# Attention and MLP in one launch: whole MLP products in the steps without maxima, residual sums on ScalarE and GpSimd, and maxima turned by DMA alone

## The chip, the cores and the metric

The kernel runs on one core of one Trainium2 chip. The core has TensorE (PE, matrix products), VectorE (DVE), ScalarE (ACT) and GpSimd (POOL), each with its own instruction queue, and SyncE (SP), whose queue issues nearly all DMAs. The metric is the device time of one execution in microseconds (us), the median of several runs.

## The reference

A pre-normalized transformer layer for 2048 tokens of width 512: 32 heads of 16, a softmax over all keys, then an MLP of width 1792 with SiLU.

```python
x = A_x
h = x + _A_ref(_layernorm(x, axis=-1), A_wqkv, A_wo)      # qkv, softmax(q k^T * scale) v, wo
h2 = h + _B_ref(_layernorm(h, axis=-1), B_w1, B_w2)       # silu(h @ w1) @ w2
return h2
```

## The kernel before, in words

**Items, steps, blocks.** The queries are cut into four blocks of 512. An item is one block with four heads, so there are 32 items (`i`), eight to a block. An item has 16 steps (`c`), one for each 128 keys; the loop at L1421 runs over all 512 steps (`g` = 16 i + c). In a step PE computes four score tiles (`scores`, L489: 128 keys by 512 queries, on one half of the array's rows, since a head's operands take 64 partitions), ACT takes their exponentials (`weigh`, into `pt`), and PE multiplies the exponentials of two steps earlier with the values (`values`, L887; LAG is 2), four heads side by side in 32 columns each. The last item (`LAST`, i = 31) is split otherwise: its first eight steps treat two heads, its last eight the other two.

**Maxima.** The softmax needs an upper bound per query. So each score is computed a second time, with queries on partitions, and DVE reduces each 128x512 tile to its maxima (`maximum`, L291, reduce at L307). There are 64 such tiles per item, 2048 in all, and they run some items ahead of the scores. They use the half of PE's rows that a score leaves free. When all of an item's maxima (a piece; in the last item a piece is half an item) are found, `finish_max` (L314) reduces them further and splits them into two fp16 rows on DVE and POOL. Then the rows must be turned (transposed) and copied into the rows of `qs`. There are two ways. `place_far` (L350) turns by a DMA (SP) and copies by two DMAs a step later. `place_max` (L368) turns on PE, copies out of PSUM on DVE, and copies by two DMAs a step later. `found_maxima` (L414) chooses: far pieces take `place_far`, near ones are put into `late` and take `place_max`. A piece is near if its first step is at most 3 steps away, at most 6 in the items of FIRSTS, or if it is a half piece of the last item. While a piece is in `late`, `maxima` (L1390) allows one maximum less in that step (`late_now`).

**Order.** All engines' instructions keep the order of the program text. `maxima(g)` decides how many maxima a step takes: 3 in most steps; in the steps of `beside` 4, or 5 where fewer than 64 + 4 (g + LEAD) are done, with LEAD 4. Callbacks wait in `agenda` (`soon(n, fn)` runs fn n steps later, at the step's start).

**The output stages.** In items 8, 16 and 24 (FIRSTS) the block just finished is projected with wo, in steps c = 9 to 15 (`output`, L1261, with n = c - 9). For n < 4 it multiplies the rows of a fourth of the block with wo (12 whole-row products into one PSUM bank, with three more maxima, MORE, after the sixth), adds x on DVE (`add_rows`, L1075), takes the statistics (`statistics`, L222: two DVE operations, then two small POOL operations for `rs`, 1/sigma), normalizes the rows of the call before on DVE (into `hx`), and splits normalized rows into a high and a low fp16 half (`split_normal`, L1081: copy on ACT, low half on POOL, for the last rows on DVE). `turn_beside` (L131) turns both halves into `hts` by a DMA on SP. Besides, `split_rows` (L1043) prepares the next rows of the attention's output in c = 10 and 11, a copy on ACT and a low half on POOL, ahead of `output`.

**The MLP beside the attention.** For the first three blocks the MLP runs in the steps of `beside`: 112 steps from the fifth step (c = 4) of the item after the output stage, or to the end, 404 to 511, for the third. Products are cut into halves of 64 rows (`half_product`, L1187), so that one half of the array works on the MLP and the other on scores or maxima (`beside_products`, L1212): on even steps the upper half of a product, on odd steps the lower half, 6 (or 7) per step. A chain of products fills one PSUM bank: 12 for each of 14 slices of the first matrix, 42 for each of four row groups of the second. In the third block the last two chains have 7 per step, so that the chain of rows 2 runs in steps 488 to 499 and that of rows 3 in 500 to 511. When a chain ends, ACT copies the bank (`g`), and later steps do the rest on ACT and POOL. Scores then have three PSUM banks, maxima three.

**The end.** After the last step `finish_last` (L1288) finishes the last item and does the fourth block's projection and MLP alone.

The functions that the diff touches, and what calls them:

Of the kernel before, what the change touches and what calls it, by code (L numbers as in the profile page):

```python
# [10 lines left out]
F32 = mybir.dt.float32  # L11
# [9 lines left out]
P = 128  # L21
# [70 lines left out]
def attention_mlp_kernel(ctx: ExitStack, tc: tile.TileContext, x, wqkv, wo, w1, w2, out):  # L92
# [19 lines left out]
    def act(fn, *a, **k):  # L112
        ins = getattr(nc.scalar, fn)(*a, **k)  # L113
        pin(ins)
        return ins

    def after(ins, earlier):

        tc.add_manual_dep(ins.ins, earlier.ins.name, mybir.DependencyInfo(
            mybir.DependencyClass.Sync, mybir.DependencyReason.DATA), reason="row halves in one bank")  # L120

    def dve(fn, *a, **k):
        pin(getattr(nc.vector, fn)(*a, **k))  # L123
# [4 lines left out]
    def dma(*a):  # L128
        pin(nc.sync.dma_start(*a))
# [155 lines left out]
    def start_of(piece):  # L285
        i, a = piece
        return KC * i + HALF * (a or 0)
# [61 lines left out]

    def place_far(piece):  # L350

        i, _ = piece
        mt = small.tile([P, P], F16, name="mt", bufs=1)
        pin(nc.sync.dma_start(mt, wide.pop(piece), transpose=True))
        split.pop(piece)

        def out():
            for j in range(2):
                rows = qs[i % RING][64 * j + 48:64 * j + 50].rearrange("r a n -> r (a n)")
                dma(rows.rearrange("r (a b) -> r a b", b=P), mt[16 * j:16 * j + 16, :])  # L360
            placed.add(piece)

        if at["attention"]:
            soon(1, out)
        else:
            out()
# [22 lines left out]
                           key=lambda t: (t[1], t[3]) if i < 2 else t[3])  # L389
            for i in range(ITEMS) for j in range(2)}  # L390
    END = 64 * ITEMS
    at = {"item": 0, "done": 0, "half": 0, "step": 0, "due": 0, "attention": False, "group": None, "ready": 0, "next": 0, "piece": 0, "blocks": True}
    agenda, late = {}, {}

    def soon(steps, fn, *a):

        agenda.setdefault(at["step"] + steps, []).append((fn, a))
# [16 lines left out]
    def found_maxima(piece):  # L414
        g = at["group"]
        output = g is not None and g // KC in FIRSTS
        if g is None or piece[1] is None and start_of(piece) - g > FAR + 3 * output:
            soon(WAIT + 1 if g is None else CALM if g > FIRSTS[0] * KC else CALM + 1, place_far, piece)
            finish_max(piece, g is not None and g > FIRSTS[0] * KC)
            return  # L420
        late.setdefault(at["step"] + (1 if output else WAIT), []).append(piece)
        unfinished.append(piece)
        found_at["step"] = at["step"]

# [61 lines left out]
    def pt_tile(name, second, dtype=F32):  # L486
        return bp.tile([P, 512], dtype, tag=f"pt{second}", name=name, bufs=PTS[second])

    def scores(g, k, kind="st"):  # L489

        i = g // KC
        a, j, c = head(g, k)
        assert piece_of(i, a) in placed
        ps = bank(kind)
        mm(ps, ks[i % RING][64 * j:64 * j + 64, a, c * P:(c + 1) * P], qs[i % RING][64 * j:64 * j + 64, a, :],
           start=True, stop=True)

        def weigh():
            pts[g, k] = pt_tile("pt", g % 2 if g in beside else k // 2)
            return act("activation", pts[g, k], ps, AF.Exp, scale=qk_f)  # L500

        return weigh
# [569 lines left out]
    def rows_of(b, t):  # L1072
        return ot[b % 2][:, t].rearrange("p c n -> p (c n)")

    def add_rows(b, t, ps):  # L1075

        dve("scalar_tensor_tensor", rows_of(b, t), ps, wo_f, hx[t], op0=ALU.mult, op1=ALU.add)

    halves = {}

    def split_normal(t):  # L1081
        rows, halves[t] = hx.pop(t), gates[:, FC - 4 + t]
        act("copy", halves[t][:, 0], rows)
        low(halves[t][:, 1], rows, halves[t][:, 0], "pool" if t < 3 else "dve")

    def gate(ps, engine="dve"):
        g, parts = zp.tile([P, 512], F32, name="g"), parts_of(pt_tile("gh", 1))
# [99 lines left out]
    def half_product(j):  # L1187
# [10 lines left out]
            after(ins, current.pop("fence"))  # L1198
        current["half"][j] += 1

    def imbalance(left, side, others, same):

        rest = [left[j] - (same if j == side else others) for j in range(2)]
        worst = max(0, -min(rest))
        while sum(rest) > 0:
            side = 1 - side
            rest[1 - side] -= 3
            rest[side] -= 1
            worst = max(worst, -min(rest) if sum(rest) >= 0 else 0)
        return worst  # L1210

    def beside_products(g, n):  # L1212

        if not current:
            count, share, of, end = chains.pop(0)
            current.update(count=count, share=share, of=of, end=end, half=[0, 0], open=[], gone=0)
# [24 lines left out]
        for m in range(max(len(other), len(same))):  # L1241
            for kind, x in same[m:m + 1] + other[m:m + 1]:
                if kind == "score":
                    weigh = scores(*x)
                    if current.get("fence", True) is None:
                        current["fence"] = weigh()
                    else:
                        weigh()
                elif kind == "max":
                    one_max(x)  # L1250
                elif kind == "half":
                    half_product(x)
# [7 lines left out]

    def output(b, n):  # L1261

        if n < 4:
            ps = bank()
            weave(project_rows(n, ps), {6: lambda: singles(MORE[n])})
            add_rows(b, n, ps)
        t = n - 3
        if t in halves:
            turn_beside(hts, slice(t * P, (t + 1) * P), halves.pop(t))
        t = n - 2  # L1270
        if 0 <= t < 4:
            split_normal(t)
            if t == 3:
                turn_beside(hts, slice(t * P, (t + 1) * P), halves.pop(t))
        if 0 < n < 5:
            normalize(hx[n - 1], rows_of(b, n - 1), *found.pop(n - 1))

        if n < 4:
            found[n] = statistics(rows_of(b, n), LN)

    O = ot[(NB - 1) % 2]

# [138 lines left out]
    for g in range(groups):  # L1421
# [45 lines left out]
        at["group"] = g  # L1467
        n = maxima(g)

        if g in beside:  # L1470
            beside_products(g, n)
        else:
            half = 1 - head(g, g % 2)[1]
            j = next_item()
            more = len(todo[j, half]) - len(todo[j, 1 - half]) if j < ITEMS else 0
            slots = range(n)
            if n == 3 and more < 0:
                slots = range(1, 4)
# [55 lines left out]
```

## Time and profile before

| | |
|---|---|
| median of 3 runs | 1562.98 us (1562.96 to 1563.38) |
| the profiled execution | 1562.87 us, span 1561.1 us |
| mean granted TensorE clock | 1.000 |
| DVE, maxima of one tile (L307) | 1842, 1146.7 us, 683 ns each |
| ACT, exponentials (pt) | 2048, 1049.1 us, 607 ns each |
| PE, scores | 2048, 639.7 us |
| PE, scores for maxima | 2048, 671.9 us |
| PE, values (pt, va) | 4096, 538.6 us |
| PE, half products of the MLP | 1008 + 1008 |

How to read it: busy time of one engine overlaps that of the others, and matmuls overlap each other (0.38 us each, but a new one can begin every 0.2 us). A duration of an instruction on DVE, ACT or POOL also contains its start, which overlaps the end of the one before; what one more costs is the distance from start to start. The chain of waits goes back from the last instruction, at each step to what released it, and so says which engine set the time in each stretch. A merged row, "x4", stands for four instructions in a row. In the rows `L99` is the helper of all matmuls, `L113` that of all ACT operations, `L123` and `L106` those of DVE and POOL, so that tiles tell operations apart: `w<-ot,mv,rs` is the normalization in an output stage, `ot<-ps,factors,w` the sum with x, `st` and `mv` the statistics, `rs` 1/sigma, `gates<-w,gates` the low half of normalized rows (`gates<-ot,gates` of the attention's output), `ps<-qs,ks` a score tile (64*128) and `ps<-ks,qs` one for the maxima (48*128), `ps<-w,gates` a half product.

### The profile page before, as it was taken

How to read it: one execution, taken by the hardware profiler on the slowest of the kernel's cores; microseconds unless marked ns; L12 is line 12 of the kernel's file. 1: busy time of each engine (PE TensorE's matmuls, PEld its weight loads, DVE VectorE, ACT ScalarE, POOL GpSimd, SP SyncE). 2: the span in 40 equal slices, each digit the busy share in tenths (PEclk: the TensorE clock that was granted, in tenths of full speed). 3: DMA queues.
4: the chain of work that ended last, by engine and by line, in shares of the span. 5: the costliest groups of instructions: out<-in, count | busy, mean ns of one | idle time of the engine just before them, and what ended most of it. 6: DMA issues, size and time to landing. Idle time of an engine off the chain costs nothing.

```text
span 1561.1 us, 30995 instructions
## 1 busy us (share of the span) xinstructions
PE 1548.6 (99%) x11483; PEld 500.0 (32%) x11483; DVE 1376.0 (88%) x2188; ACT 1232.9 (79%) x2404; POOL 553.8 (35%) x761
## 2 busy tenths in 40 slices
PE   9999999999999999999999999999999999999999
PEld 6433322222222333333322333333322333332354
DVE  7999999999999999999999999999999999993322
ACT  6545799999977889888868998888868989888532
POOL 6643444554532354311142544310142445211100
PEclk9999999999999999999999999999999999999999
DMA  6667423333433122344433211444432221335322
GB/s 219 171 171 234 140 80 96 99 112 94 119 89 93 31 57 61 108 128 142 141 78 86 57 45 49 129 141 130 120 97 69 56 62 48 91 107 172 97 88 75
DMA packets 136260, 163.18 MB, mean 105 GB/s; under 512 B 43312, under 2 KB 80240, under 8 KB 136108
## 3 DMA queue, kind: packets, MB, share of 16 engines
q1 hardware_dynamic: 131356, 152.68, 33.9%
q10 hardware_dynamic: 4752, 8.52, 2.0%
q8 instruction: 90, 1.47, 0.4%
q14 instruction: 62, 0.51, 0.1%
HBM read 126.48 MB, written 24.63 MB: 97 GB/s over the span
## 4 chain that ended last, share of the span: by engine, by line
PE 88%; DVE 8%; ACT 2%; issue 1%; POOL 0%; POOLq 0%; ACTq 0%
PE ps L99 87%; DVE mx L307 5%; ACT pt L113 1%; DVE mx L305 1%; PE ps L102 1%; DVE w L123 0%; DVE st L123 0%; DVE ot L123 0%; DVE pvs L123 0%; POOL wv_l L106 0%; ACT g L113 0%; ACT pvs L113 0%; DVE xtl L123 0%; DVE ks L123 0%; POOL rs L106 0%
## 5 line engine op out<-in xcount | busy, mean ns | idle before, releaser
L307 DVE TENSOR_REDUCE mx<-ps 128x1 f32<-128x512 f32 x1842 | 1146.7, 683 | 58.7 <-PE ps L99 26.5
L113 ACT ACTIVATE pt<-ps 128x512 f32<-128x512 f32 x2048 | 1049.1, 607 | 179.3 <-PE ps L99 177.4
L99 PE MATMUL ps<-ks,qs 48*128 48x512 f16 x2048 | 671.9, 380 | 5.2 <-DVE mx L307 2.4
L99 PE MATMUL ps<-qs,ks 64*128 64x512 f16 x2048 | 639.7, 377 | 0.6
L99 PE MATMUL ps<-pt,va 128*17 128x512 f32 x4096 | 538.6, 598 | 0.6
L99 PE MATMUL ps<-hts,w 64*128 64x512 f16 (+2 forms) x1212 | 285.0, 372 | 0.0
L99 PE MATMUL ps<-w,gates 64*128 64x512 f16 x1008 | 245.6, 378 | 0.1
L99 PEld LDWEIGHTS <-ks 64*128 64x128 f16 x2048 | 177.0, 94 | 207.6 <-issue 163.2
L99 PEld LDWEIGHTS <-qs 48*128 48x128 f16 x2048 | 167.1, 94 | 69.1 <-issue 29.2
L99 PEld LDWEIGHTS <-w 64*128 64x128 f16 (+1 forms) x1212 | 101.6, 95 | 236.9 <-ACT pt L113 107.2
L99 PEld LDWEIGHTS <-gates 64*128 64x128 f16 (+1 forms) x1152 | 95.1, 94 | 240.2 <-ACT pt L113 112.7
L106 POOL TENSOR_TENSOR ri<-rc,minus 128x16 f32<-128x16 f32 x31 | 90.7, 2926 | 220.8 <-DMA rc<-dn 220.8
L99 PEld LDWEIGHTS ps<-pt,va 128*17 128x17 f32 x4096 | 68.2, 95 | 204.1 <-issue 196.3
L305 DVE TENSOR_REDUCE mx<-ps 128x2 f32<-128x1024 f32 x103 | 119.1, 1219 | 4.3 <-PE ps L99 3.5
L106 POOL TENSOR_SCALAR t<-t,factors 128x512 f32<-128x512 f32 x42 | 29.1, 693 | 190.5 <-ACT t L113 190.5
L113 ACT ACTIVATE g<-ps,factors 128x512 f32<-128x512 f32 x68 | 47.0, 692 | 42.6 <-PE ps L99 42.6
L106 POOL TENSOR_TENSOR ot<-ot,g 128x512 f32<-128x512 f32 x12 | 15.3, 1272 | 122.5 <-ACT g L113 122.5
L113 ACT ACTIVATE ks<-ps 128x512 f32<-128x512 f32 x30 | 17.9, 597 | 50.2 <-PE ps L99 43.9
L123 DVE SCALAR_TENSOR_TENSOR gh<-g,factors,gh 128x512 f16<-128x512 f32 x14 | 10.5, 751 | 52.1 <-ACT gh L113 52.1
L106 POOL TENSOR_TENSOR t<-t,g 128x512 f32<-128x512 f32 x42 | 53.7, 1278 | 3.5
L106 POOL TENSOR_TENSOR sl<-ks,sh 128x512 f16<-128x512 f32 x30 | 34.6, 1155 | 50.5 <-ACT sh L113 32.2
L106 POOL TENSOR_SCALAR nm<-nm 128x16 f32<-128x16 f32 (+1 forms) x42 | 10.8, 257 | 112.4 <-DVE nm L321 108.2
(160 smaller groups left out, 1025.7 us busy)
## 6 DMA issues: line engine op xcount, KB each, us to landing
w<-w2d SPq DMA_DIRECT2D x182, 256.0 KB
ks<-kd SPq DMA_DIRECT2D x120, 192.0 KB
w<-w1d SPq DMA_DIRECT2D x56, 256.0 KB
ks<-in_B_w_dram ACTq DMA_DIRECT2D x28, 256.0 KB
w<-in_B_w_dram SPq DMA_DIRECT2D x28, 256.0 KB
qs<-qd SPq DMA_DIRECT2D x128, 48.0 KB
kd<-sh SPq DMA_DIRECT2D x16, 256.0 KB
qd<-sh SPq DMA_DIRECT2D x16, 256.0 KB
```

The costliest lines, as they stand in the source:

```text
L99: return tc.keep_in_program_order(nc.tensor.matmul(*a, **k))
L102: tc.keep_in_program_order(nc.tensor.transpose(*a))
L106: tc.keep_in_program_order(getattr(nc.gpsimd, op)(*a, **k))
L113: ins = getattr(nc.scalar, fn)(*a, **k)
L123: pin(getattr(nc.vector, fn)(*a, **k))
L305: pin(nc.vector.tensor_reduce(of, space[:, n:n + 2, :], axis=AX.X, op=ALU.max))
L307: pin(nc.vector.tensor_reduce(of[:, j:j + 1], space[:, n, :], axis=AX.X, op=ALU.max))
```

## The change

Three things. (1) In `found_maxima` the choice goes by distance alone (more than 3 steps), so that half pieces and near pieces of the output stages take `place_far`, in an output stage one step after they are found. (2) In `output` ACT multiplies the projected rows by wo_f into SBUF and POOL adds x, behind the normalization of the rows before (`after`); the statistics of these rows move to the start of the next call; the last rows are normalized one call later, split two calls later (their turn comes in the next item's first step); the halves of rows 2 and 3 are copied by POOL, not ACT, and all low halves are POOL's. (3) In the steps of `beside` where no maxima are left and the current product is complete in both halves, `beside_scores` issues the step's four scores and then as many whole-row products as spread the rest evenly over the steps left (all but the last); two of the maxima's PSUM banks go to the scores.

```diff
@@ found_maxima
-        if g is None or piece[1] is None and start_of(piece) - g > FAR + 3 * output:
-            soon(WAIT + 1 if g is None else CALM if g > FIRSTS[0] * KC else CALM + 1, place_far, piece)
+        if g is None or start_of(piece) - g > FAR:
+            soon(WAIT + 1 if g is None else 1 if output else CALM if g > FIRSTS[0] * KC else CALM + 1, place_far, piece)
             finish_max(piece, g is not None and g > FIRSTS[0] * KC)
             return
-        late.setdefault(at["step"] + (1 if output else WAIT), []).append(piece)
+        late.setdefault(at["step"] + WAIT, []).append(piece)
@@ place_far
-        i, _ = piece
+        i, a = piece
+        n = 16 if a is None else 8
...
-                rows = qs[i % RING][64 * j + 48:64 * j + 50].rearrange("r a n -> r (a n)")
-                dma(rows.rearrange("r (a b) -> r a b", b=P), mt[16 * j:16 * j + 16, :])
+                rows = qs[i % RING][64 * j + 48:64 * j + 50, slice(None) if a is None else slice(a, a + 1)]
+                dma(rows.rearrange("r a n -> r (a n)").rearrange("r (a b) -> r a b", b=P), mt[n * j:n * j + n, :])
@@ weigh
-            pts[g, k] = pt_tile("pt", g % 2 if g in beside else k // 2)
+            pts[g, k] = pt_tile("pt", g % 2 if g in beside and not at["alone"] else k // 2)
@@ split_normal
-        act("copy", halves[t][:, 0], rows)
-        low(halves[t][:, 1], rows, halves[t][:, 0], "pool" if t < 3 else "dve")
+        if t < 2:
+            act("copy", halves[t][:, 0], rows)
+        else:
+            pool("tensor_copy", halves[t][:, 0], rows)
+        low(halves[t][:, 1], rows, halves[t][:, 0], "pool")
@@ new
+    def whole_products(count):
+        for _ in range(count):
+            lhs, rhs = next(current["of"])
+            ins = mm(space[:, at["bank"], :], lhs, rhs, start=current["half"] == [0, 0], stop=current["half"][0] == current["count"] - 1)
...
+            current["half"] = [n + 1 for n in current["half"]]
+            current["gone"] += 1
+        if current["gone"] == current["count"]:
+            current["end"](space[:, at["bank"], :])
+            current.clear()
+
+    def beside_scores(g):
+
+        if not current:
+            begin_chain()
+        rest = current["count"] - current["gone"] + sum(count for count, *_ in chains)
+        groups_left = max(beside) - g
+        for k in range(4):
+            scores(g, k ^ (g % 2))()
+        whole_products(min(current["count"] - current["gone"], -(-rest // groups_left)))
@@ output
+        if 0 < n < 5:
+            found[n - 1] = statistics(rows_of(b, n - 1), LN)
         if n < 4:
             ps = bank()
             weave(project_rows(n, ps), {6: lambda: singles(MORE[n])})
-            add_rows(b, n, ps)
+            if n:
+                mv, rs = found.pop(n - 1)
+                norm = nc.vector.tensor_scalar(hx[n - 1], rows_of(b, n - 1), mv[:, 0:1], rs, op0=ALU.subtract, op1=ALU.mult)
+                pin(norm)
+            z = zp.tile([P, 512], F32, name="g")
+            act("mul", z, ps, wo_f)
+            add = nc.gpsimd.tensor_tensor(rows_of(b, n), z, hx[n], ALU.add)
+            pin(add)
+            if n:
+                after(add, norm)
         t = n - 3
         if t in halves:
-            turn_beside(hts, slice(t * P, (t + 1) * P), halves.pop(t))
-        t = n - 2
-        if 0 <= t < 4:
+            turn_half(t)
+        for t in {2: (0,), 3: (1,), 4: (2,), 6: (3,)}.get(n, ()):
             split_normal(t)
             if t == 3:
-                turn_beside(hts, slice(t * P, (t + 1) * P), halves.pop(t))
-        if 0 < n < 5:
-            normalize(hx[n - 1], rows_of(b, n - 1), *found.pop(n - 1))
-
-        if n < 4:
-            found[n] = statistics(rows_of(b, n), LN)
+                soon(1, turn_half, t)
+        if n == 5:
+            normalize(hx[3], rows_of(b, 3), *found.pop(3))
+
+    def turn_half(t):
+        turn_beside(hts, slice(t * P, (t + 1) * P), halves.pop(t))
@@ the loop over steps
-        if g in beside:
+        if g in beside and next_item() == ITEMS and (at["alone"] or current and current["half"][0] == current["half"][1]):
+            if not at["alone"]:
+                at["alone"] = True
+                banks["st"] += banks["sm"][:2]
+                banks["sm"] = banks["sm"][2:]
+            if chains or current:
+                beside_scores(g)
+            else:
+                for k in range(4):
+                    scores(g, k ^ (g % 2))()
+        elif g in beside:
             beside_products(g, n)
```

More of the change, by code (lines that the diff above doesn't have):

```diff
@@ L119, in after @@
         tc.add_manual_dep(ins.ins, earlier.ins.name, mybir.DependencyInfo(
-            mybir.DependencyClass.Sync, mybir.DependencyReason.DATA), reason="row halves in one bank")
+            mybir.DependencyClass.Sync, mybir.DependencyReason.DATA), reason="order")
     def dve(fn, *a, **k):
@@ L391, in attention_mlp_kernel @@
     END = 64 * ITEMS
-    at = {"item": 0, "done": 0, "half": 0, "step": 0, "due": 0, "attention": False, "group": None, "ready": 0, "next": 0, "piece": 0, "blocks": True}
+    at = {"item": 0, "done": 0, "half": 0, "step": 0, "due": 0, "attention": False, "group": None, "ready": 0, "next": 0, "piece": 0, "blocks": True, "alone": False}
     agenda, late = {}, {}
@@ L1073, in rows_of @@
         return ot[b % 2][:, t].rearrange("p c n -> p (c n)")
-    def add_rows(b, t, ps):
-        dve("scalar_tensor_tensor", rows_of(b, t), ps, wo_f, hx[t], op0=ALU.mult, op1=ALU.add)
     halves = {}
@@ L1199, in half_product, with begin_chain @@
         current["half"][j] += 1
+    def whole_products(count):
+        for _ in range(count):
+            lhs, rhs = next(current["of"])
+            ins = mm(space[:, at["bank"], :], lhs, rhs, start=current["half"] == [0, 0], stop=current["half"][0] == current["count"] - 1)
+            if "fence" in current:
+                after(ins, current.pop("fence"))
+            current["half"] = [n + 1 for n in current["half"]]
[11 more added lines that the diff above has]
+        whole_products(min(current["count"] - current["gone"], -(-rest // groups_left)))
+    def begin_chain():
+        count, share, of, end = chains.pop(0)
+        current.update(count=count, share=share, of=of, end=end, half=[0, 0], open=[], gone=0)
     def imbalance(left, side, others, same):
@@ L1214, in beside_products @@
         if not current:
-            count, share, of, end = chains.pop(0)
-            current.update(count=count, share=share, of=of, end=end, half=[0, 0], open=[], gone=0)
+            begin_chain()
         side = g % 2
```

## The prediction

> **What bounds the kernel now.** I read the page first, then the chain of waits, then the timelines of the stretches that the diff touches.
>
> ```profile
> span 1561.1 us, 30995 instructions
> PE 88%; DVE 8%; ACT 2%; issue 1%; POOL 0%; POOLq 0%; ACTq 0%
> ```
>
> TensorE (PE) carries the end almost everywhere, VectorE (DVE) for 8% of the span, ScalarE (ACT) for 2%. POOL (GpSimd) is as good as never on the chain. So work moved to POOL or ACT is worth something only in the DVE pieces of the chain, and PE work removed is worth its own time. The profiled execution took 1562.87 us, 1.77 more than its span and 0.11 below the median; I sum differences and take them from the median 1562.98. About 0.2% (3.1 us) is what a measurement can tell from no change.
>
> A step is one pass of the loop over g; c is its number within an item. Each step shows as a burst of four exps on ACT, so bursts mark steps. The three output stages (blocks 1, 2, 3 in order of time) project rows in c9 to c12, finish the normalization after that, and begin the MLP beside the attention at c4 of the next item.
>
> ```profile
> 454.87 2.07 ACT L113 ACTIVATE pt<-ps 128x512 f32<-128x512 f32 x4 [3.31 <-PE ps L99]
> 471.81 2.06 ACT L113 ACTIVATE pt<-ps 128x512 f32<-128x512 f32 x4 [3.15 <-PE ps L99]
> 487.66 3.08 DVE mx L307 x5
> 801.69 2.06 ACT L113 ACTIVATE pt<-ps 128x512 f32<-128x512 f32 x4 [3.31 <-PE ps L99]
> 818.52 2.06 ACT L113 ACTIVATE pt<-ps 128x512 f32<-128x512 f32 x4 [2.81 <-PE ps L99]
> 835.09 1.29 DVE mx L307 x2
> 1147.44 2.07 ACT L113 ACTIVATE pt<-ps 128x512 f32<-128x512 f32 x4 [3.31 <-PE ps L99]
> 1164.04 2.07 ACT L113 ACTIVATE pt<-ps 128x512 f32<-128x512 f32 x4 [2.81 <-PE ps L99]
> 1180.61 1.29 DVE mx L307 x2
> ```
>
> In each block the first row is c10, the second c13, the third the first reduce of c4. So c10 to c12 take 16.94, 16.83 and 16.60 us, and the seven steps c13 to c3 take 15.85, 16.57 and 16.57. From c4 on, as the chain's row for block 1 shows, a step costs five reduces of DVE, 3.08.
>
> **c10 to c12, the row sums.** What PE needs alone is seen at the start of block 3's stage, before DVE falls behind (upper rows of the timeline of PE; the lower ones are a step near the end of the attention):
>
> ```profile
> 1142.71 0.59 PE L99 MATMUL ps<-wo_h,gates 128*128 128x512 f16 x2
> 1143.36 0.59 PE L99 MATMUL ps<-wo_h,gates 128*128 128x512 f16 x2
> 1143.79 0.38 PE L99 MATMUL ps<-wo_l,gates 128*128 128x512 f16 x1
> 1144.10 0.60 PE L99 MATMUL ps<-ks,qs 48*128 48x512 f16 x3
> 1144.63 0.60 PE L99 MATMUL ps<-wo_h,gates 128*128 128x512 f16 x2
> 1148.09 0.59 PE L99 MATMUL ps<-wo_h,gates 128*128 128x512 f16 x2
> ...
> 1441.41 0.39 PE L99 MATMUL ps<-w,gates 64*128 64x512 f16 x1
> 1442.71 0.38 PE L99 MATMUL ps<-w,gates 64*128 64x512 f16 x1
> 1443.02 1.05 PE L99 MATMUL ps<-pt,va 128*17 128x512 f32 x8
> 1444.03 0.39 PE L99 MATMUL ps<-w,gates 64*128 64x512 f16 x1
> ```
>
> From projection to projection it is 1148.09 − 1142.71 = 5.38, with whole-row products 0.215 apart (two between 1143.36 and 1143.79). Three such steps are 16.14, so DVE costs 0.80, 0.69 and 0.46 there. What DVE does is shown by block 2 at the end of c12, and in c13 and c14:
>
> ```profile
> 817.41 0.74 DVE L123 SCALAR_TENSOR_TENSOR ot<-ps,factors,w 128x512 f32<-128x512 f32 x1
> 818.07 0.54 DVE L123 TENSOR_SCALAR w<-ot,mv,rs 128x512 f32<-128x512 f32 x1
> 818.52 0.69 DVE L123 BATCH_NORM_STATS2 st<-ot 128x6 f32<-128x512 f32 x1
> 819.24 0.18 DVE L123 BATCH_NORM_AGGREGATE mv<-st 128x2 f32<-128x6 f32 x1
> 819.34 1.85 DVE L307 TENSOR_REDUCE mx<-ps 128x1 f32<-128x512 f32 x3
> 821.11 1.50 DVE L123 TENSOR_SCALAR w<-ot,mv,rs 128x512 f32<-128x512 f32 x1
> 822.53 1.88 DVE L307 TENSOR_REDUCE mx<-ps 128x1 f32<-128x512 f32 x3
> 824.33 0.68 DVE L123 TENSOR_TENSOR gates<-w,gates 128x512 f16<-128x512 f32 x1
> 824.93 0.68 DVE L307 TENSOR_REDUCE mx<-ps 128x1 f32<-128x512 f32 x1
> ```
>
> By start-to-start spacing a step has six reduces (2 × 1.8 = 3.6), the sum 0.66, the normalization 0.45 and the statistics 0.82: 5.5, over PE's 5.38. Without the sum it is 4.9, and PE becomes the bound at 5.38. The sum's new way:
>
> ```profile
> L113 ACT ACTIVATE g<-ps,factors 128x512 f32<-128x512 f32 x68 | 47.0, 692 | 42.6 <-PE ps L99 42.6
> L106 POOL TENSOR_TENSOR ot<-ot,g 128x512 f32<-128x512 f32 x12 | 15.3, 1272 | 122.5 <-ACT g L113 122.5
> L106 POOL CAST gates<-t 128x512 f16<-128x512 f32 x42 | 25.6, 610 | 2.7
> ```
>
> It takes 0.69 on ACT and 1.27 on POOL, 2.0 after the projection. Its reader, the statistics, now stands behind the next step's three reduces, about 2.9 after the projection (values 1.01, from 1443.02 to 1444.03, then 1.85 of reduces), so the sum is hidden by some 0.9. ACT stands idle 2.8 to 3.3 before each burst in those rows, so its 0.69 costs nothing. The sum on POOL waits for the normalization before it; behind it in POOL's queue lie a low half (one of the costs below) and the next two small operations for 1/sigma, which the next normalization needs 1.9 or more after the statistics. The tightest place is c11, where split_rows puts a low half ahead of them: I find about 0.1 to spare. If that cover is gone, DVE waits and PE with it (a rival below). I take the whole 0.80 + 0.69 + 0.46 = **2.0**; bounds 0 and 2.0.
>
> **c13 to c3, the end of the normalization.** Counted from c13's first exp (818.52), the reduces of c13 begin 0.8 late now, since sum, normalization and statistics stand ahead of them. After the change that 0.8 is gone, but the statistics (0.82) stand behind these reduces instead: nothing won. The low half on DVE, 0.60 by spacing (824.33 to 824.93), goes to POOL: 0.6 won. The normalization of the last rows is the costly one: 1.50 rather than 0.54. POOL tells why:
>
> ```profile
> 819.51 0.19 POOL L106 TENSOR_SCALAR rs<-mv 128x1 f32<-128x1 f32 x1 [2.56 <-DVE mv L123]
> 819.79 0.56 POOL L106 TENSOR_TENSOR rs<-rs,expos 128x1 f32<-128x1 f32 x1
> 821.17 1.16 POOL L106 TENSOR_TENSOR gates<-w,gates 128x512 f16<-128x512 f32 x1 [0.82 <-ACT gates L113]
> ```
>
> It lies beside a low half on POOL and both end together. After the change, counted from c13's exps: reduces 0.05 to 1.85, statistics, mv at 2.57, 1/sigma on POOL to 3.7, the copy that came from ACT (0.61) to 4.35, low half from 4.45 to 5.6. On DVE the next reduces run from 2.67, so the normalization starts at 4.45 as well. They meet again, and it stays 1.5. So blocks 2 and 3 win 0.6 each. Block 1 escapes the collision today, and one reduce is missing in its c13:
>
> ```profile
> 473.81 0.53 DVE L123 TENSOR_SCALAR w<-ot,mv,rs 128x512 f32<-128x512 f32 x1
> ```
>
> Its 15.85 becomes the others' 16.0: 0.1 lost. Sum **1.1**; bounds −0.4 (each block's 0.6 eaten, block 1 at 16.3) and 3.9 (no collision).
>
> The Trainium skill, page "SBUF — State Buffer", section "Who interferes with whom", has it that such a DVE operation and a GpSimd one take a shared port pair in turn, and that the first to issue holds it. By that rule a normalization that starts first would keep its 0.54 (1551.2 as the sum). The trace does not bear it out: at 821.11 the normalization started 0.06 ahead of POOL and still paid.
>
> Two things move on SP's queue. The last rows' halves are turned by DMA in c0 rather than c14; c4, which reads them, comes four steps of 2.3 (16.0 / 7) later, 9 us: free, and if it is not, c4's first products wait. The turned maxima now pass SP twice, the second time behind the turn of rows 1, which waits for POOL's low half. In block 1 they are issued about 5 us after c13's exps; c0 begins at 6, but DVE's late reduces hold its last maximum until 8, so that I take them as covered. Uncovered they cost up to 1 in block 1.
>
> **Maxima.** A piece that waited to be turned by TensorE took one maximum out of a step (late_now). Each output stage then started the MLP one short and paid one more five-reduce step. Now 3.08 instead of 2.62 (tail rows below, also seven slots) for one step less per block: 3 × 0.46 = **1.4**. The same hiccup before the end:
>
> ```profile
> 1398.55 2.07 ACT L113 ACTIVATE pt<-ps 128x512 f32<-128x512 f32 x4 [0.55 <-PE ps L99]
> 1401.70 1.09 ACT L113 ACTIVATE pt<-ps 128x512 f32<-128x512 f32 x2 [1.08 <-PE ps L99]
> ```
>
> That step is 3.15 where its neighbours are 2.6: **0.5**. The turns' own work on PE and DVE lies inside these differences.
>
> **The tail.** By the target in the code (64 + 4 × (g + 4) maxima before step g) all 2048 are done at step 492, which leaves twenty steps. A step there (the lower PE rows) is seven half products at 0.217, with four scores in the other half of the array, 0.31 to the values, 1.01 to the next step: 2.62. After: four scores in pairs (2 × 0.215), a change to whole rows, n products at 0.215, values. The change to whole rows is priced by the three 48-row maxima at 1144.10, which fill two slots: 1144.63 − 1144.10 − 0.215 = 0.31, or 0.09 over a slot. With n = 4: 0.215 + 0.31 + 0.645 + 0.31 + 1.01 = 2.49; with n = 3: 2.27. Left at step 492 are 28 + 42 products over 19 steps, each taking the rest divided by the steps left, rounded up: n = 4 in 13 steps, 3 in six, none in the last. That wins 13 × 0.13 + 6 × 0.35 = 3.8. ACT needs 2.06 per step and now has 0.2 to 0.4 left for two evictions of 0.69 and a copy: 0.1 to 0.2 worse. The last step saves 1.1 on PE, but its values wait for its exps: 0.4. Five score banks let each step's scores go out at once. Sum **4.0**; bounds 1.5 (each step at 2.6) and 5.
>
> The Trainium skill, page "TensorEngine Tiling (Array Packing)", section "Key Properties", warns that changing the tiling mode drains TensorE, which speaks against this part. The trace agrees with 0.09 a change; were the drain a whole matmul's 0.38, 19 more of them would take back 5.5.
>
> **Sum.** 2.0 + 1.1 + 1.4 + 0.5 + 4.0 = 9.0: 1562.98 − 9.0 = **1554.0**.
>
> **The rivals.**
> *No collision*: the normalization gets in ahead of POOL's low half or between copy and low half. 0.95 per block more, −11.8: 1551.2. For it: the tie is 0.01 us by my sums. Against: both collisions on record. 20%.
> *The tail gives little*: ACT's queue or the scores' banks hold each step near 2.55, or whole products are not entered at step 492 because a product is half done (against this: 14 of 42 are done on both sides). −5 to −6.5: about 1557. 17%.
> *GpSimd becomes the bound* (the slower side): POOL's order puts a sum (1.27) or low half ahead of 1/sigma, and each of the three following normalizations of a block waits x. It costs 9x; from x = 1.0 the gain is gone, at a whole sum and its gap, 1.4, it gives −9.0 + 12.6: 1566.6. For it: c11's 0.1. Against: POOL is idle 2.6 us before 1/sigma in the row. 6%.
> *No change*: PE binds the output stages anyway and half the tail is lost: −1 to −3, about 1561. 6%.
>
> **How the numbers follow.** The forecast has 51%. The range 1550.5 to 1558.0 takes in the first two rivals; the slower and the unchanged case stay outside. Faster by over 0.2%: 0.51 + 0.20 + 0.17 = 0.88; same 0.06; slower 0.06.
>
> **What would show it.** Right: c10 to c12 at 5.38 a step with no DVE in the chain; one five-reduce step less in each block; bursts at 2.49 and 2.27 in the tail; normalizations of 1.5 in c14. Wrong: DVE waiting for rs in c11, scores of c0 waiting for a DMA on qs, bursts still 2.6 apart after the last reduce, or a span above 1559.

## The result and the profile after

| | before | after |
|---|---|---|
| median | 1563.02 us (1562.92 to 1563.38, 6 runs) | 1553.76 us (1553.58 to 1554.09, 6 runs) |
| ratio after / before, 95% interval | | 0.9941 [0.9928, 0.9954] |
| profiled execution, and its span | 1562.87 us, 1561.1 us | 1553.58 us, 1551.7 us |

The change saves 9.26 us; the forecast was 1554.0. The page of after answers the two lines of before:

```profile
span 1551.7 us, 30864 instructions
PE 91%; DVE 6%; ACT 2%; issue 1%; POOL 0%; DMA 0%; SPq 0%; POOLq 0%; ACTq 0%
```

VectorE's share of the chain has fallen from 8% to 6%, TensorE has taken it over, and neither GpSimd nor ScalarE carries more of it. The chain of waits through the output stage of block 1 shows where DVE went (short pieces of "issue" between the rows are left out):

```profile
450.24 5.35 PE ps L99 x30
455.62 5.35 PE ps L99 x30
460.99 5.35 PE ps L99 x30
466.37 4.74 PE ps L99 x25
471.13 1.89 DVE mx L307 x3
...
475.61 2.24 DMA qs<-mt
477.90 2.73 PE ps L99 x17
...
486.93 3.08 DVE mx L307 x5
```

The steps c10 to c12 are pure PE at 5.38 from start to start, with nothing of DVE between them. ACT's part of the sum (`g`) has gone into the idle time of 3.31 that stood ahead of c10's exps: 2.08 are left ahead of `g`, and 0.55 between `g` and the exps (timeline of ACT):

```profile
453.73 0.69 ACT L113 ACTIVATE g<-ps,factors 128x512 f32<-128x512 f32 x1 [2.08 <-PE ps L99]
454.97 2.06 ACT L113 ACTIVATE pt<-ps 128x512 f32<-128x512 f32 x4 [0.55 <-PE ps L99]
```

In the chain a new link has come in: PE waits for the copy of the turned maxima (`qs<-mt`) before c0 can begin. Block 2 has one exception, in c12, where the chain goes through ACT:

```profile
809.87 0.69 ACT g L113
810.55 0.51 ACT gates L113
811.06 0.51 ACT pt L113
811.61 9.47 PE ps L99 x58
```

`g` and a copy stand ahead of the step's exps there, and the step takes 5.51 rather than 5.38. The same two stand there in blocks 1 and 3, where the step takes 5.38. In block 3 `g` starts 0.48 after the start of the projection's last product (1153.25 to 1153.73), in block 2 0.76 after it (809.11 to 809.87); what held it there the profile does not show.

In the groups of instructions, kept apart by shape, the normalization splits into the nine that `output` issues under a projection and the three of the last rows, issued in c14 (columns: busy us, mean ns of one, idle before):

```profile
L1295 DVE TENSOR_SCALAR w<-ot,mv,rs 128x512 f32<-128x512 f32 x9 | 4.9, 540 | 0.6 <-POOL rs L106 0.5
L123 DVE TENSOR_SCALAR w<-ot,mv,rs 128x512 f32<-128x512 f32 x3 | 4.0, 1320 | 0.0
```

The last rows still pay, 1.32 rather than 0.54. In the tail, the timeline of PE shows the new steps: four scores, then four or three whole-row products, then the values.

```profile
1438.85 1.05 PE L99 MATMUL ps<-pt,va 128*17 128x512 f32 x8
1439.84 0.60 PE L99 MATMUL ps<-qs,ks 64*128 64x512 f16 x4
1440.38 1.04 PE L99 MATMUL ps<-w,gates 128*128 128x512 f16 x4
1441.34 1.05 PE L99 MATMUL ps<-pt,va 128*17 128x512 f32 x8
...
1442.87 0.82 PE L99 MATMUL ps<-w,gates 128*128 128x512 f16 x3
1443.62 1.05 PE L99 MATMUL ps<-pt,va 128*17 128x512 f32 x8
1445.89 0.62 PE L99 MATMUL ps<-pt,va 128*17 128x512 f32 x4
```

From values to values that is 2.49 with four products (1438.85 to 1441.34) and 2.27 with three (1443.62 to 1445.89).

The same reading of all steps gives the account by stage. A step ends with its values products (`ps<-pt,va`, of the exps of two steps earlier), so each number is the time between the first values products that close two steps in the timeline of PE. The tail runs from the values of step 489, at the end of step 491, to the start of the last two copies of the attention's output (`pvs`).

| stage | before | after | won | forecast |
|---|---|---|---|---|
| c10 to c12, blocks 1, 2, 3 | 16.94, 16.83, 16.60 | 16.13, 16.27, 16.13 | 1.84 | 2.0 |
| c13 to c3 | 15.82, 16.53, 16.53 | 15.80, 15.99, 15.98 | 1.11 | 1.1 |
| c4 to c15 | 35.24, 33.81, 33.81 | 34.75, 33.32, 33.32 | 1.47 | 1.4 |
| steps 483 to 491 | 25.10 | 24.60 | 0.50 | 0.5 |
| tail | 56.52 | 52.33 | 4.19 | 4.0 |

They add up to 9.11 of the 9.4 by which the spans differ. In the chain, steps of five reduces (3.08 each) number six in block 1 and three in blocks 2 and 3, against seven, four and four before.

### The profile page after: what moved, and what is told of

Its sections match the earlier page's. It is cut to its first block, busy times and chain, and to the rows that moved or that the text cites. A ratio compares the mean times of both kernels' runs of the same rounds, so it can differ in the third digit from the quotient of the medians.

```text
span 1551.7 us, 30864 instructions
## 1 busy us (share of the span) xinstructions
PE 1539.4 (99%) x11408; PEld 495.2 (32%) x11408; DVE 1365.7 (88%) x2168; ACT 1237.9 (80%) x2410; POOL 575.4 (37%) x782
## 4 chain that ended last, share of the span: by engine, by line
PE 91%; DVE 6%; ACT 2%; issue 1%; POOL 0%; DMA 0%; SPq 0%; POOLq 0%; ACTq 0%
PE ps L99 90%; DVE mx L307 3%; DVE mx L305 1%; ACT pt L113 1%; PE ps L102 1%; DVE pvs L123 0%; DMA ks<-in_A_x_dram 0%; DVE st L123 0%; POOL wv_l L106 0%; DVE ks L123 0%; ACT g L113 0%; POOL rs L106 0%; DMA qs<-mt 0%; ACT pvs L113 0%; DVE ot L123 0%
## 5 line engine op out<-in xcount | busy, mean ns | idle before, releaser
L99 PE MATMUL ps<-qs,ks 64*128 64x512 f16 x2048 | 626.8, 377 | 1.3 <-DMA qs<-mt 0.7
L99 PEld LDWEIGHTS <-ks 64*128 64x128 f16 x2048 | 173.0, 94 | 221.7 <-issue 175.3
L99 PE MATMUL ps<-w,gates 64*128 64x512 f16 (+1 forms) x938 | 230.3, 378 | 0.2 <-ACT g L113 0.2
L99 PEld LDWEIGHTS <-gates 64*128 64x128 f16 (+1 forms) x1082 | 88.8, 95 | 223.0 <-ACT pt L113 97.8
L113 ACT ACTIVATE g<-ps,factors 128x512 f32<-128x512 f32 x80 | 55.2, 690 | 64.7 <-PE ps L99 59.7
```

Source lines behind the costliest of these rows:

```text
L99: return tc.keep_in_program_order(nc.tensor.matmul(*a, **k))
```

## The experiments

None of them leaves out a part of the reference. The theory is the forecast's: five separate savings, each with a mechanism of its own. Ratios are against the kernel before and have intervals of ±0.0013, about 2 us, so neighbouring kernels are told apart by the stage times of their traces and by medians whose ranges stay apart; where ranges overlap the text says so. The kernel before, run beside them, had medians of 1562.89 to 1563.02. Edits are made to the kernel after, unless another is named.

**e1: the third part undone.** Half products to the end.

```diff
-        if g in beside and next_item() == ITEMS and (at["alone"] or current and current["half"][0] == current["half"][1]):
+        if False:
```

> The changed kernel without its third part: the last twenty steps run half products as before. Theory (the parts add up, and the tail is worth what its steps show, 53.7 before and 49.0 after): 4.7 us over the changed kernel, 1558.5, with bursts 2.6 apart again after the last reduce. Rival (the tail's gain is in part a later wait taken away elsewhere, or ACT's pace hides it): 2 us or less, 1555.8.

1557.82 us (1557.75 to 1558.37), ratio 0.9967 [0.9955, 0.998]: 4.06 above after. All stages up to step 491 are as after within 0.01, and the tail is back at 56.52. In the timeline of ACT the bursts are 2.61 to 2.65 apart again, and ACT waits for scores ahead of each:

```profile
1441.99 2.06 ACT L113 ACTIVATE pt<-ps 128x512 f32<-128x512 f32 x4 [0.58 <-PE ps L99]
1444.64 2.06 ACT L113 ACTIVATE pt<-ps 128x512 f32<-128x512 f32 x4 [0.58 <-PE ps L99]
```

The tail's 4.19 belongs to the third part alone. Its two halves, the whole products and the two more banks for scores, were not tried apart.

**e2: the output stages as before.** `output`, `split_normal` and `add_rows` from the kernel before; the maxima and the tail stay changed.

```diff
-            z = zp.tile([P, 512], F32, name="g")
-            act("mul", z, ps, wo_f)
-            add = nc.gpsimd.tensor_tensor(rows_of(b, n), z, hx[n], ALU.add)
...
+            add_rows(b, n, ps)
```

> The changed kernel without its second part: sums, splits and turns of the output stages as before (sum on DVE). Theory: c10 to c12 go back to 16.6 to 16.9 us per block (1.8 in all) and c13 to c3 to about 16.5 in each block, now with three reduces in c13 everywhere (1.1 to 1.7): 2.9 to 3.5 us over the changed kernel, 1556.7 to 1557.3. Rival (the stages gain from the maxima alone): under 1 us, 1554.5.

1557.16 us (1556.8 to 1557.33), 0.9962 [0.9949, 0.9976]: 3.40 above after. In the chain DVE is back in c11 and c12:

```profile
459.98 0.54 DVE w L123
460.51 0.61 DVE st L123
...
461.33 1.78 DVE mx L307 x3
```

c10 to c12 take 17.19, 17.58 and 17.58, 3.82 more than after and 1.98 more than before. In blocks 2 and 3 two things lengthen c12: `late_now` no longer takes a maximum out of it, so DVE, the bound there, has one reduce more, and a normalization (812.05) collides with a low half on POOL that started 0.29 ahead, and takes 1.15 rather than 0.54. c13 to c3 take 15.81 in all blocks, 0.34 less than after in sum and 0.72 less than before in blocks 2 and 3. There the normalization of the last rows starts 0.18 ahead of the low half and keeps its 0.54, while the low half takes 1.39 (DVE, then POOL):

```profile
821.42 0.54 DVE L123 TENSOR_SCALAR w<-ot,mv,rs 128x512 f32<-128x512 f32 x1
```

```profile
821.60 1.39 POOL L106 TENSOR_TENSOR gates<-w,gates 128x512 f16<-128x512 f32 x1 [0.94 <-ACT gates L113]
```

So the total lies in the expected range by two misses that cancel: c10 to c12 lost twice the 1.8 expected, and c13 to c3 did not go back to about 16.5. The second part as a whole is worth 3.40 beside the new maxima. The sum on ScalarE and GpSimd was not undone by itself.

**e3: the first part undone.** `found_maxima` as before, so that near pieces are turned on PE.

```diff
-        if g is None or start_of(piece) - g > FAR:
+        if g is None or piece[1] is None and start_of(piece) - g > FAR + 3 * output:
...
-        late.setdefault(at["step"] + WAIT, []).append(piece)
+        late.setdefault(at["step"] + (1 if output else WAIT), []).append(piece)
```

> The changed kernel without its first part: near pieces turned by PE, with one maximum less in the step where they wait. Theory: one five-reduce step more per block (3 x 0.47) and the step of 3.1 before the end (0.5), less about 0.4 that block 1 gains in c13 by a missing reduce: 1.5 to 1.9 us over the changed kernel, 1555.4. Rival (the turns by DMA win nothing, or cost block 1 its wait for qs): 0 to 0.5, 1554.0.

1555.06 us (1554.91 to 1555.59), 0.995 [0.9936, 0.9964]: 1.30 above after. c4 to c15 take 35.24, 33.81, 33.81 again and steps 483 to 491 25.09, the values of before. But c13 to c3 are shorter than after, by 0.48 in block 1, where one reduce is missing in c13: there the account is nil. In blocks 2 and 3 the reduce is missing in c12, and PE waits there for the piece that it turns (0.27 at 811.41): c10 to c12 take 16.33 each, 0.06 and 0.20 more than after, and c13 to c3 0.18 less. The maxima's term stands in its own stages; what it is worth to the whole is 1.3.

**e4: the copy of rows 2 behind the normalization of rows 3.** DVE's operation then runs with nothing beside it on POOL. The turn of rows 2 goes one step later with the copy.

```diff
+            copy = nc.gpsimd.tensor_copy(halves[t][:, 0], rows)
+            pin(copy)
+            if behind is not None:
+                after(copy, behind)
...
-        for t in {2: (0,), 3: (1,), 4: (2,), 6: (3,)}.get(n, ()):
-            split_normal(t)
-            if t == 3:
-                soon(1, turn_half, t)
+        norm = None
         if n == 5:
-            normalize(hx[3], rows_of(b, 3), *found.pop(3))
+            mv, rs = found.pop(3)
+            norm = nc.vector.tensor_scalar(hx[3], rows_of(b, 3), mv[:, 0:1], rs, op0=ALU.subtract, op1=ALU.mult)
+            pin(norm)
+        for t in {2: (0,), 3: (1,), 5: (2,), 6: (3,)}.get(n, ()):
+            split_normal(t, norm)
+            if t > 1:
+                soon(1, turn_half, t)
```

> The changed kernel with POOL's copy and low half of rows 2 put behind the normalization of rows 3, so that the two cannot meet in c14. Theory: the normalization falls from 1.3 to 1.5 us to 0.54 and blocks 2 and 3 win 0.85 each in c13 to c3; block 1 wins at most 0.2, since there c0's scores wait for the DMA into qs until 477.9 whatever DVE does: 1.7 to 1.9 us under the changed kernel, 1552.0. Rival A (the collision is covered): no change, 1553.8. Rival B (no DMA wait of its own in block 1): 2.6 under, 1551.2.

1551.67 us (1551.55 to 1552.12), 0.9928 [0.9914, 0.9941]: 2.09 below after. In block 2 the normalization is short again (timeline of DVE), and POOL's copy begins behind it, at 821.57:

```profile
820.90 0.54 DVE L1312 TENSOR_SCALAR w<-ot,mv,rs 128x512 f32<-128x512 f32 x1
```

For comparison after, DVE and then POOL at the same place:

```profile
820.95 1.32 DVE L123 TENSOR_SCALAR w<-ot,mv,rs 128x512 f32<-128x512 f32 x1
```

```profile
820.14 0.61 POOL L106 CAST gates<-w 128x512 f16<-128x512 f32 x1
820.83 1.16 POOL L106 TENSOR_TENSOR gates<-w,gates 128x512 f16<-128x512 f32 x1
```

After, the low half starts 0.12 ahead of the normalization and ends at 821.99; the normalization ends 0.28 later, at 822.27. Without the collision it takes 0.54, and c13 to c3 fall from 15.99 to 15.20 in blocks 2 and 3, 0.79 each: the whole 1.32 − 0.54 = 0.78. Block 1 gives only 0.33, because something else is next: c0 waits for the turned maxima in e4 as it does after. That wait was taken up by e8.

**e5: the sum free of the normalization.** It tells whether the order that `after` sets is needed.

```diff
-            if n:
-                after(add, norm)
```

> The changed kernel without the wait of POOL's sum for the normalization before it. Theory (the sum waits longer for ACT's copy than for the normalization, in the profile after its last releaser is ACT nearly every time): the same order of events, 1553.8 within 0.3. Rival (the wait is what keeps the two apart): sums meet normalizations in c10 to c12, each then takes 1.3 to 1.5 instead of 0.55, 0.25 of it covered by DVE's idle time: nine times 0.6, 1559.

1555.74 us (1555.53 to 1556.0), 0.9953 [0.9939, 0.9966]: 1.98 above after. c10 to c12 take 16.73, 16.86 and 16.73, 0.6 more in each block. Neither theory had it quite: of three pairs in a block only one collides as thought. DVE and POOL in block 1:

```profile
459.96 1.63 DVE L1295 TENSOR_SCALAR w<-ot,mv,rs 128x512 f32<-128x512 f32 x1 [0.25 <-POOL rs L106]
465.89 0.54 DVE L1295 TENSOR_SCALAR w<-ot,mv,rs 128x512 f32<-128x512 f32 x1
```

```profile
460.05 1.26 POOL L1299 TENSOR_TENSOR ot<-g,w 128x512 f32<-128x512 f32 x1
466.08 1.47 POOL L1299 TENSOR_TENSOR ot<-g,w 128x512 f32<-128x512 f32 x1 [0.78 <-ACT g L113]
```

At 459.96 the sum came 0.09 behind the normalization, and the normalization took 1.63. At 465.89 it came 0.19 behind, the normalization kept its 0.54, and the sum took 1.47 rather than 1.26. So a lead of 0.09 did not save the normalization here, and one of 0.19 did. `after` buys 0.6 a block by keeping the first pair apart.

**e6: the scores in two groups.** Two scores, half of the whole products, two scores, the other half: two changes more between half rows and whole rows in each tail step, the same work.

```diff
-        for k in range(4):
+        for k in range(2):
             scores(g, k ^ (g % 2))()
+        whole_products(n // 2)
+        for k in range(2, 4):
+            scores(g, k ^ (g % 2))()
+        whole_products(n - n // 2)
```

> The changed kernel, in the tail two scores, half of the step's whole products, two scores, the other half: two more changes between half rows and whole rows in each of 19 steps, no other work. Theory (a change costs 0.1 over the slot, in both directions): 0.2 a step, 3.6 in all, 1557.4, bursts about 2.7 and 2.5 apart. Rival A (only the first change after scores costs, the rest overlaps): 1.8, 1555.6. Rival B (a change drains for a whole matmul, 0.38): 14 us, 1568.

1557.49 us (1557.45 to 1557.94), 0.9964 [0.9951, 0.9978]: 3.73 above after. The tail takes 56.17, 3.84 more, over 19 steps 0.20 each. In the timeline of PE a step with four products takes 2.70 (1422.70 to 1425.40) instead of 2.49:

```profile
1422.70 1.05 PE L99 MATMUL ps<-pt,va 128*17 128x512 f32 x8
1423.69 0.39 PE L99 MATMUL ps<-qs,ks 64*128 64x512 f16 x2
1424.01 0.61 PE L99 MATMUL ps<-w,gates 128*128 128x512 f16 x2
1424.55 0.39 PE L99 MATMUL ps<-qs,ks 64*128 64x512 f16 x2
...
1425.40 1.05 PE L99 MATMUL ps<-pt,va 128*17 128x512 f32 x8
```

From the first whole products to the next scores it is 0.54, two slots of 0.215 and 0.11; a change costs 0.1, in both directions. Nearly all of the tail's gain, 3.84 of 4.19, depends on the scores going together.

**e7: the turns on PE, but no maximum left out.** e3 with one line more. If the number of maxima were all that the turns cost, it would be as fast as after.

```diff
-        late_now = at["step"] in late
+        late_now = False
```

> The third experiment (near pieces turned by PE) with the rule taken out that allows one maximum less while a piece waits. Theory (the first part's gain is the count of maxima, not the turn itself): back to the changed kernel but for the turns' own 0.15 on PE, five times, 1554.0 to 1554.4, and seven, four and four five-reduce steps. Rival (the turn on PE and its copy on DVE cost): 1555.0, as with the rule.

1555.13 us (1554.85 to 1555.64), 0.9949 [0.9936, 0.9963]: as slow as e3, the ranges overlap, and the theory missed. c4 to c15 take 34.75, 33.33 and 33.33, after's times, so the five-reduce step is gone again, and the time went elsewhere. c13 to c3 are as long as after again, 0.96 more than in e3 in sum, and c10 to c12 take 16.61 in blocks 2 and 3, 0.56 more than in e3 in sum. The timeline of PE in c12 of block 2:

```profile
811.37 0.38 PE L99 MATMUL ps<-ks,qs 48*128 48x512 f16 x1
812.09 0.22 PE L102 MATMUL ps<-ident_h,ns 128*32 128x128 f16 x1 [0.35 <-DVE mx L307]
```

`place_max` takes one of the maxima's three PSUM banks, and PE waits for DVE to reduce what lies in it. So in c12 the maximum that `late_now` left out was the price of a bank free in time, and over the whole run it paid about as much as it cost. The DMA turn needs neither.

**e8: e4, and every turn of rows one step later.** The diff is to e4. The theory is that in block 1 the copies of the maxima stand behind the turn of rows 1 on SP's queue.

```diff
         if t in halves:
-            turn_half(t)
+            soon(1, turn_half, t)
```

> The fourth experiment with each turn of a normalized half issued one step later, at the step's start, so that in block 1 the DMAs into qs stand ahead of the turn of rows 1 on SP's queue. Theory (that turn holds them back, and c0 waits for them): block 1's c0 falls from 2.70 to about 2.25, 0.4 to 0.5 under the fourth experiment, 1551.2. Rival (their own time from issue to landing holds c0, or DVE does): 1551.7, no change.

1551.42 us (1551.15 to 1551.98), 0.9925 [0.9912, 0.9939], with a range that overlaps e4's. SP's queue after, and then in e8:

```profile
473.49 1.26 SPq L133 DMA_TRANSPOSE hts<-gates  x1
474.85 1.41 SPq L129 DMA_DIRECT2D qs<-mt  x2
```

```profile
472.87 1.41 SPq L129 DMA_DIRECT2D qs<-mt  x2
474.39 1.25 SPq L133 DMA_TRANSPOSE hts<-gates  x1
```

The copies go out 1.98 earlier, PE no longer waits for them, and c13 to c3 of block 1 fall from e4's 15.47 to 15.02. So the queue held c0. The median shows 0.25 of that 0.45: in the profiled execution, the slowest of the five, the tail is 0.53 longer (52.86), by a late load that is taken up in the last section.

**e9: e8, with the last rows normalized by POOL.** Nothing of these rows is left on DVE but the statistics; the copy of rows 2 stands behind the normalization by the queue alone.

```diff
-        norm = None
-        if n == 5:
-            mv, rs = found.pop(3)
-            norm = nc.vector.tensor_scalar(hx[3], rows_of(b, 3), mv[:, 0:1], rs, op0=ALU.subtract, op1=ALU.mult)
-            pin(norm)
+        if n == 4:
+            normalize(hx[3], rows_of(b, 3), *found.pop(3), engine="pool")
```

> The eighth experiment with the normalization of rows 3 on POOL (2.1 us there before, in another place), ahead of its copy of rows 2, and off DVE. Theory (what is left over 14.1 us in c13 to c3 is DVE's statistics and normalization between the reduces, 0.8 and 0.5): c13 to c3 falls from 15.2 to about 14.7 in each block, 1.2 to 1.5 under the eighth, 1550.0. Rival (POOL ends the halves of rows 3 too late for c4's first products, or the statistics alone hold the banks): no gain or up to 3 us more, 1551.4 to 1554.

1550.69 us (1550.58 to 1551.16), 0.9922 [0.9908, 0.9935]: the fastest of all, 3.07 below after. It costs POOL 2.08 (timeline of POOL), which hides:

```profile
819.38 2.08 POOL L106 TENSOR_SCALAR w<-ot,mv,rs 128x512 f32<-128x512 f32 x1
```

c13 to c3 are 14.73, 14.91 and 14.91, 0.29 below e8 in each block. That is less than DVE's 0.45 from start to start, and 0.87 in sum rather than the 1.2 to 1.5 expected. In the chain of block 2 the exps of c0 now stand where e8 has PE alone, so something else is next:

```profile
820.17 1.94 PE ps L99 x12
822.11 2.63 ACT pt L113 x6
```

**e10: the low half a little later.** Two small memsets ahead of POOL's copy of rows 2 shift the low half by about 0.2, so that the normalization starts first. Nothing is set in order.

```diff
+    spare = small.tile([P, 16], F32, name="spare", bufs=1)
...
+            if t == 2:
+                for _ in range(2):
+                    pool("memset", spare, 0.0)
             pool("tensor_copy", halves[t][:, 0], rows)
```

> The changed kernel with two idle operations of about 0.2 us each on POOL ahead of its copy of rows 2 in c13, so that its low half starts about 0.4 us after the normalization of rows 3 instead of 0.1 before; the two still lie beside each other. Theory (whoever is first by more than the start of an operation keeps its time, as in the fifth experiment): the normalization takes 0.54, the low half 1.3 to 1.6, and blocks 2 and 3 win as in the fourth experiment: 1551.7 to 1552.2. Rival (lying beside each other is what costs, as the prediction read it): 1.3 to 1.5 for the normalization and 1553.8.

1551.79 us (1551.54 to 1552.12), 0.9928 [0.9914, 0.9941]: as e4. DVE and POOL in block 2:

```profile
821.39 0.54 DVE L123 TENSOR_SCALAR w<-ot,mv,rs 128x512 f32<-128x512 f32 x1
```

```profile
820.57 0.28 POOL L106 MEMSET spare<- 128x16 f32 x2
...
821.48 1.47 POOL L106 TENSOR_TENSOR gates<-w,gates 128x512 f16<-128x512 f32 x1
```

The low half starts 0.09 behind the normalization and now pays itself, 1.47 rather than 1.16, while DVE's takes 0.54. c13 to c3 fall to 15.61 in block 1 and 15.20 in blocks 2 and 3. The two still lie beside each other; which one starts first is worth 0.79 a block in blocks 2 and 3.

## Why the prediction was right

**c10 to c12** (forecast 2.0, measured 1.84). PE alone sets these steps at 5.38, and e2 shows that taking the second part back puts DVE into them again. The cover of the sum on POOL held, 1/sigma in c11 included. What is missing is in block 2's c12, at 5.51: "so its 0.69 costs nothing" was read off ACT's long idle time before the bursts. That held while `g` stood alone in it. In c12 a copy of normalized rows stands between `g` and the exps, and where `g` began late, in block 2, nothing was left to cover it.

**c13 to c3** (1.1, measured 1.11). The low half's 0.6 a block fits blocks 2 and 3 (0.54 and 0.55), and e2 supports its size: with the low half on DVE and the normalization short these steps take 15.81, in e4, with the low half on POOL and the normalization short, 15.20. The collision stayed, and e4 prices it at 0.79. That the sum is met so closely is in part luck. The normalization fell from 1.50 to 1.32, which the forecast did not count and which does not show in the stage; why is open. In block 1 the "0.1 lost" was 0.02 won, and one of the prediction's signs of being wrong did appear there: c0's scores wait for a DMA on `qs`. The maxima's copies, taken "as covered", stand in the chain, and PE waits 0.67 for them. What that wait costs while the collision lasts was not tried; without the collision it is 0.45 (e4 against e8).

**The sentence on the shared port was wrong**, and the forecast took the right branch partly by luck: its sums had the two starts tied to 0.01, and in the changed kernel POOL came 0.12 first. It called 821.11 against the rule, since the normalization there started 0.06 ahead of POOL and still paid. But the trace of before also held the opposite case, earlier in the same block (DVE, then POOL):

```profile
812.57 0.54 DVE L123 TENSOR_SCALAR w<-ot,mv,rs 128x512 f32<-128x512 f32 x1
```

```profile
812.78 1.34 POOL L106 TENSOR_TENSOR gates<-w,gates 128x512 f16<-128x512 f32 x1
```

With a lead of 0.21 the normalization kept its 0.54, and the low half took 1.34 rather than 1.16. e2, e5 and e10 show the same with leads of 0.18, 0.19 and 0.09. Leads of 0.06 (821.11) and 0.09 (459.96 in e5) were lost, so the record of a start is not yet the moment that decides. Nor do the two "end together": at 821.11 POOL ends at 822.33 and DVE at 822.61, and in each collision that DVE lost it ended 0.28 after POOL. The Trainium skill, page "SBUF — State Buffer", section "Who interferes with whom", says that where a DVE operation needs the port pair that it shares with GpSimd, the one that issues first keeps the pair until it is done. The changed kernel, e2 and e10 agree, with 1.32 where POOL started first and 0.54 where DVE did; the lost leads of before and e5 are the exception.

**Maxima and hiccup** (1.4 + 0.5, measured 1.47 + 0.50). One five-reduce step less in each block, as forecast. What the forecast did not see is that `late_now` had bought a free bank in c12 (e7). It makes no difference to this sum, but whoever keeps the turns on PE and only deletes the rule gains nothing.

**The tail** (4.0, measured 4.19). Steps of 2.49 and 2.27 as forecast, and e1 gives the same 4.06 to 4.19 from the other side. The rival that ACT's queue or the banks hold a step at 2.55 is out. The price of a change of mode, 0.09 from one row of before, is confirmed by two more changes in each step (e6: 0.1 each). The Trainium skill, page "TensorEngine Tiling (Array Packing)", section "Key Properties", has the drain without a price, and here it is a quarter of a matmul's 0.38.

The parts add nearly: undone one by one they cost 4.06 + 3.40 + 1.30 = 8.76 of 9.26. As e2's 3.40 holds a gain and a loss of its own, it is in part chance that the sum comes so close.

## What to carry to other kernels

When work leaves an engine, read what that engine was hiding: here taking DVE's collision away won block 1 only 0.33, because a DMA late in SP's queue was next, and moving that won 0.45 more. Two operations of DVE and GpSimd that overlap are not settled by "they collide": look which starts first, because the loser waits for the other, and let the engine that is not on the chain be the loser. A saving that is restored in one stage and lost in the next (e7) is only seen with a table by stage, not in the total.

## What the runs showed of the hardware

Three things were not expected. The first is how long a lead must be. Over all twelve traces, with the recorded starts taken unrounded and POOL operations of 128x512 alone, DVE's normalization lost with leads of 52 and 57 ns (before) and of 74, 74 and 84 ns (e5), and won with each lead from 88 ns (e10) upward. So in these pairs of operations the border lies at 84 to 88 ns; whether it lies there for other operations, these runs don't say. The second: in c12 PE's whole queue, products and scores behind it included, was held 0.35 by one small turn that needed a bank still unread by DVE (e7).

And the last loads of the second matrix can come late. In e8 the chain of waits goes through one in the tail:

```profile
1429.05 5.32 DMA w<-w2d
```

That step takes 3.02 in e8, and 3.22 in e9, and the tails are 0.53 and 0.73 longer than after's 52.33. In the program's order these loads stand on SP behind the transfers of the last attention outputs. That alone does not make them late: after issues the same load in the same place, at 1431.23, 22.53 after its tail begins, as e8 does (22.52), and is not held. What delayed the landing in e8 is open. Whether an earlier load would bring e9 lower still was not tried.
